# A fused attention and FFN kernel: opening reordered, masks in fp16, warm-up matmuls, values fixed up one chunk earlier

## The chip, the core and the metric

The kernel runs on one core of one Trainium2 chip. The metric is the device time in microseconds (us) of one execution. The kernel was timed several times on each chip, and medians are quoted. All runs named here are fast: none is more than 1.5% above the fastest run of its kernel.

The times of the kernel before fall into two groups, about 264.9 to 265.7 us and about 266.8 to 268.2 us, so its median moves between 265.4 and 267.5 us with the share of each group. The profiled run of it took 267.2 us, so its trace is of the slower group. What sets the groups apart was not found. Experiments are therefore compared in microseconds with the median of the changed kernel (240.16 us, and 240.05 us when it was run again in another call), and not by their ratios to the kernel before.

## The reference, cut to what matters

```python
# q, k, v: (4 batches, 8 heads, 768 positions, 64) fp32;  w_in (512, 2048), w_out (2048, 512)
scores = q @ k.T / 8
keep   = (key < 8) | ((0 <= rel) & (rel < 96))        # 8 global keys, and a band of 96
bias   = -slope[h] * where(is_global & ~is_local, 96, abs(rel))
a      = softmax(where(keep, scores + bias, -1e9))
x      = (a @ v), heads side by side                  # 3072 tokens x 512
out    = (relu(x @ w_in) ** 2) @ w_out                # fp32, 3072 x 512
```

The kernel computes the exponential of the scores and multiplies it by a mask, `exp(-slope * distance)`, built once and zero where `keep` is false.

## The kernel before

The 3072 tokens are cut into 12 chunks of 256, three to a batch. Each chunk goes through these jobs, each a Python closure that emits instructions; in the traces each engine runs what is emitted for it in that order (TensorE's weight loads may go ahead): before, the first copy of q waited on VectorE until 7.38 us, behind the masks, though its transposes started at 5.64 us. The jobs are:

- `load`: q, k, v from HBM, issued by GpSimd (names of tiles: `sq`, `sk`, `sv`);
- `turn_q`, `turn_k`: TensorE transposes (`trq`, `trk`), ScalarE or VectorE copies to `qx`, `kx`, VectorE copies beside them (`kb` for chunks that are not the first of a batch);
- `fix_v`: VectorE copies the values into `vodd`, and, for the eight chunks that are not the first of a batch ("shifted" below), also into `veven`, with rows of the chunk before and the global keys:

```python
        nc.vector.tensor_copy(out=odd[:, hh, :, 0:D], in_=cut(ck.sv, slice(0, P)))       # L244
        if ck.u != 0:
            nc.vector.tensor_copy(out=odd[0:GP, ...], in_=glob)                          # L248
            nc.vector.tensor_copy(out=even[0:HP, ...], in_=cut(ck.sv, slice(0, HP)))     # L249
            nc.vector.tensor_copy(out=even[HP:P, ...], in_=cut(pre.sv, slice(HP, P)))    # L250
            nc.vector.tensor_copy(out=even[HP:HP + GP, ...], in_=glob)                   # L251
```

- `att[c][0..7]`: two batches of scores (`sp` on TensorE, `ex` on ScalarE, `phat = ex * mask` on VectorE); four attends (`av` on TensorE, then `rec` and `tm`, the normalisation, on VectorE); two `to_x` (`trx` on TensorE, `xt` on ScalarE);
- `f1(c)`: first FFN matmul (`hps`), relu (`hr`, ScalarE), square (`h`, VectorE); `f2(c)`: second FFN matmul (`yps`), copy, store.

FFN jobs and attention jobs of a later chunk are interleaved by `place(main, side, slots)`, which puts each side job ahead of the main job of that number. The opening and the first phase read:

```python
        fill_ident(); load(0, q); fill_index(); load(0, k); load(0, v)     # fill_index: 8 index fills on GpSimd
        load_w_in(0, 512); load(1); ...                                    # cut: the other loads
        fill_masks(); fill_dist(0, 2, 0)              # VectorE, fp32
        fill_decay(0, 2, 0, 4)                        # ScalarE: mask of heads 0 to 3
        run([turn_q(0) and turn_k(0) in halves, att[0][0],
             fill_decay(0, 2, 4, 8), fix_v(0), att[0][2], att[0][1],       # heads 4 to 7
             fill_even(), att[0][3], att[0][6], turn_q(1), att[0][4],      # even masks, VectorE
             turn_k(1), att[0][5], att[0][7], fill_decay(2, 3, 0, 8)])
        run(place(f1(0), [fix_v(1)] + [att[1][i] for i in ORDER] + prep(2),
                  [1, 0, 2, 3, 4, 5, 6, 6, 7, 6, 7]))
        ...                                           # cut: f1(1) with chunk 2, f2(0) with chunk 3
        for c in range(1, NC):                        # steady stages: f2(c) and f1(c+1) in turn
            side = [fix_v(c + 3)] + [att[c + 3][i] for i in ORDER];  slots = [2, 0, 4, 5, 7, 8, 11, 12, 15]
```

The softmax here doesn't subtract the row's maximum and nothing guards it: scores larger than these inputs give would overflow.

## Time and profile before

| | before |
|---|---|
| median | 265.4 us (265.04 to 267.4, 4 runs) |
| profiled span | 265.4 us |
| TensorE busy | 224.8 us |
| TensorE idle | 40.6 us, of it about 13.7 before the first `hps`, 3.7 after the last matmul |

From the page of the kernel before: the busy line of TensorE, and its busy share and granted clock in 40 equal slices of the span (one digit a slice, in tenths).

```profile
...
PE 224.8 (85%) x2208; PEld 155.6 (59%) x2208; DVE 156.4 (59%) x410; ACT 143.8 (54%) x255; POOL 39.7 (15%) x57
...
PE   1335579498878998999998989999989979999994
...
PEclk9999759979999999999999999999999999999999
...
```

The row "PE" shows that the second half is full and that the first quarter is not. The row "PEclk" shows a lowered clock in several slices there.

The stretches view of the kernel before gives, for each stretch, its length, the busy time and the number of instructions of TensorE, its weight loads, VectorE, ScalarE and GpSimd, then the granted clock, the DMA share and GB/s.

```profile
...
30.00:40.00 10.00, 5.61 (x50) 3.91 (x48) 6.09 (x17) 3.75 (x8) 3.40 (x4) 0.67 1.30 203
50.00:60.00 10.00, 7.02 (x74) 5.32 (x72) 6.41 (x19) 4.77 (x10) 0.00 (x0) 0.83 0.39 39
80.00:100.00 20.00, 18.85 (x194) 13.27 (x193) 14.04 (x36) 12.26 (x23) 2.63 (x3) 1.00 0.74 101
160.00:180.00 20.00, 20.00 (x212) 14.03 (x212) 12.21 (x32) 11.97 (x21) 0.00 (x0) 1.00 0.08 28
...
```

TensorE is busy 18.85 of 20 us at 80 us, but all 20 at 160 us. Between 30 and 40 us it is busy 5.61 us of 10, at a mean clock of 0.67.

The waits view of TensorE for the kernel before lists who waited for what: total us, times, longest.

```profile
...
PE av L291 <- DVE veven L251: 8.2, 8, 1.2
...
PE av L291 <- DVE vodd L248: 6.1, 6, 3.1
...
PE av L291 <- DVE vodd L244: 4.2, 2, 3.0
...
```

Here `av` waits for `fix_v`, 18.5 us behind the three copies L251, L248 and L244; 3.0 us of the last line lie in the opening. VectorE is only 59% busy in the whole, but its queue is in order: the copies for a chunk are emitted just ahead of the attend that needs them.

The chain of work that ended last shows the clock's effect (start, us, what):

```profile
...
35.34 1.71 PE hps L335 x8
37.48 1.72 PE hps L335 x8
...
86.11 0.87 PE hps L335 x8
...
```

Eight `hps` matmuls take 1.71 us near 36 us and 0.87 later. The opening, from the timeline of the kernel before (start, us, engine, line, operation, tiles, count; in brackets idle time ahead and what ended it):

```profile
...
3.79 0.90 POOL L184 DMA_DIRECT2D sk<-in_k_dram  x1
...
6.48 0.98 DVE L147 TENSOR_SCALAR dist<-dist,fill 128x512 f32<-128x512 f32 x1
...
7.38 0.40 DVE L198 COPY qx<-trq 128x512 f16<-128x512 f16 x1
7.54 1.28 ACT L151 ACT_TABLE_LOAD   x1 [7.54 <-DVE dist L147]
...
12.92 2.21 ACT L151 ACTIVATE mask<-dist 128x512 f16<-128x512 f32 x4
...
18.29 0.35 DVE L135 TENSOR_SCALAR dist<-dist_94,shift 128x256 f32<-128x256 f32 x1
...
20.46 0.42 DVE L298 TENSOR_TENSOR tm<-av,rec 128x256 f16<-128x256 f32 x1
...
26.87 3.35 PE L335 MATMUL hps<-xt,w_in_sb 128*128 128x256 f16 x16
...
```

The masks hold VectorE until 7.4 us, and only then can it copy the transposed q. The exponentials of heads 4 to 7 (12.92), the even masks (from 18.29) and then the normalisation (20.46) come before the first `hps` at 26.87 us.

### The profile page before, as it was taken

To read this page: it belongs to the slowest core of one execution; us is meant where nothing else is said; L and a number is where in the kernel's file an instruction comes from. 1 tells how busy PE (TensorE), PEld (TensorE's weight loads), DVE (VectorE), ACT (ScalarE), POOL (GpSimd) and SP (SyncE) were. 2 spreads that over 40 slices of the span, in tenths; PEclk is the share of its full clock that TensorE was granted. 3 is DMA by queue.
4 is the path that set the end of the run, shared out by engine and by line. 5 is a ranking of instruction groups with operands and counts; after the bars stand their busy time and mean duration, and the time that the engine had idled before them with its cause. 6 is when DMAs were issued, how large, how long until landed. Compare 5 with 4: busy or idle time off the path is not lost.

```text
span 265.4 us, 5380 instructions
## 1 busy us (share of the span) xinstructions
PE 224.8 (85%) x2208; PEld 155.6 (59%) x2208; DVE 156.4 (59%) x410; ACT 143.8 (54%) x255; POOL 39.7 (15%) x57
## 2 busy tenths in 40 slices
PE   1335579498878998999998989999989979999994
PEld 1224357376445765777765757777657656766651
DVE  6765357656668659547667677476486565333331
ACT  0854819549455754765674575567637635333310
POOL 8843322103031201201210200000000000000000
PEclk9999759979999999999999999999999999999999
DMA  5999999904849194284724811011101101111112
GB/s 51 175 190 198 199 202 181 154 3 45 110 52 154 41 118 42 51 111 42 103 61 77 81 40 42 0 42 41 42 0 42 40 2 41 42 40 40 42 40 79
DMA packets 45144, 20.26 MB, mean 76 GB/s; under 512 B 37952, under 2 KB 42048, under 8 KB 45120
## 3 DMA queue, kind: packets, MB, share of 16 engines
q0 software_dynamic: 41664, 13.63, 46.3%
q1 hardware_dynamic: 3456, 6.29, 6.2%
q8 instruction: 17, 0.28, 0.4%
q14 instruction: 7, 0.06, 0.1%
HBM read 27.26 MB, written 6.29 MB: 126 GB/s over the span
## 4 chain that ended last, share of the span: by engine, by line
PE 62%; DVE 17%; ACT 16%; issue 3%; POOL 1%; POOLq 0%; ACTq 0%
PE yps L347 26%; PE hps L335 25%; ACT ex L274 9%; PE av L291 5%; DVE phat L277 3%; PE sp L267 3%; ACT hr L338 2%; PE trx L310 2%; DVE vodd L244 2%; ACT mask L151 2%; DVE veven L251 1%; DVE veven L250 1%; DVE vodd L248 1%; PE trk L211 1%; ACT kx L213 1%
## 5 line engine op out<-in xcount | busy, mean ns | idle before, releaser
L335 PE MATMUL hps<-xt,w_in_sb 128*128 128x256 f16 x768 | 103.8, 281 | 0.0
L338 ACT ACTIVATE hr<-hps 128x512 f16<-128x512 f32 x96 | 58.6, 614 | 80.2 <-PE hps L335 80.0
L335 PEld LDWEIGHTS <-w_in_sb 128*128 128x128 f16 x768 | 73.8, 100 | 19.4 <-issue 0.3
L274 ACT ACTIVATE ex<-sp 128x512 f16<-128x512 f32 x96 | 49.5, 605 | 11.7 <-PE sp L267 11.7
L277 DVE TENSOR_TENSOR phat<-ex,mask 128x1024 f16<-128x1024 f16 x48 | 33.2, 692 | 28.6 <-ACT ex L274 28.6
L291 PEld LDWEIGHTS <-phat 128*128 128x128 f16 x384 | 19.0, 102 | 28.0 <-issue 9.1
L291 PE MATMUL av<-vodd,phat 128*128 128x65 f16 x256 | 19.9, 203 | 10.8 <-DVE vodd L248 6.1
L298 DVE TENSOR_TENSOR tm<-av,rec 128x256 f16<-128x256 f32 x48 | 20.4, 424 | 1.7
L312 ACT CAST xt<-trx 128x512 f16<-128x512 f32 x24 | 14.6, 607 | 10.0 <-PE trx L310 9.9
L184 POOL DMA_DIRECT2D sq<-in_q_dram x12 | 10.7, 896 | 60.7 <-PE trq L196 58.0
L351 DVE COPY y<-yps 128x512 f32<-128x512 f32 x24 | 16.4, 685 | 5.4 <-PE yps L347 5.4
L267 PE MATMUL sp<-qx,kx 64*128 64x128 f16 x256 | 15.6, 234 | 3.9 <-DVE kx L225 1.4
L291 PE MATMUL av<-veven,phat 128*128 128x65 f16 x128 | 11.5, 197 | 8.2 <-DVE veven L251 8.2
L267 PEld LDWEIGHTS <-kx 64*128 64x128 f16 x256 | 10.5, 102 | 11.4 <-issue 8.0
L184 POOL DMA_DIRECT2D sk<-in_k_dram x12 | 10.7, 891 | 39.8 <-PE trk L211 35.5
L310 PE MATMUL trx<-perm,tm 128*128 128x128 f16 x96 | 10.2, 223 | 6.6 <-DVE tm L298 6.6
L310 PEld LDWEIGHTS <-tm 128*128 128x128 f16 x96 | 7.1, 99 | 10.7 <-DVE tm L298 8.1
L196 PE MATMUL trq<-ident,sq 128*128 128x128 f16 x96 | 8.2, 234 | 5.6 <-DVE loc L143 5.6
L198 ACT COPY qx<-trq 128x1024 f16<-128x1024 f16 x11 | 11.4, 1038 | 1.9 <-PE trq L196 1.9
L213 ACT COPY kx<-trk 128x1024 f16<-128x1024 f16 x11 | 11.7, 1060 | 0.3 <-PE trk L211 0.3
L184 POOL DMA_DIRECT2D sv<-in_v_dram x12 | 10.7, 893 | 2.8 <-DMA w_out_sb<-in_moe_w_out_dram 1.3
L196 PEld LDWEIGHTS <-sq 128*128 128x128 f16 x96 | 6.8, 106 | 5.8 <-DMA sq<-in_q_dram 5.6
(85 smaller groups left out, 280.0 us busy)
## 6 DMA issues: line engine op xcount, KB each, us to landing
out_dram<-y SPq DMA_DIRECT2D x24, 256.0 KB, 2.0
sq<-in_q_dram POOLq DMA_DIRECT2D x12, 256.0 KB, 4.5
sk<-in_k_dram POOLq DMA_DIRECT2D x12, 256.0 KB, 5.6
sv<-in_v_dram POOLq DMA_DIRECT2D x12, 256.0 KB, 6.5
w_in_sb<-in_moe_w_in_dram POOLq DMA_DIRECT2D x4, 512.0 KB, 12.0
w_out_sb<-in_moe_w_out_dram POOLq DMA_DIRECT2D x4, 512.0 KB, 17.8
```

Of the source, the lines that this page charges most:

```text
L184: nc.gpsimd.dma_start(out=dst, in_=src[ck.b, :, ck.u * CH:(ck.u + 1) * CH, :].rearrange("h (p e) d -> p h (e d)", e=2))
L196: nc.tensor.transpose(out=trp[:, h, :], in_=ck.sq[:, h, :], identity=ident)
L267: nc.tensor.matmul(sp[ek][:, e, s, :], lhsT=ck.keys[rr][rows, h, :], rhs=ck.q[rows, 1 - ek:3 - ek, h, rr * HP:(rr + 1) * HP], start=True, ...
L274: nc.scalar.activation(out=ex[:, ek].rearrange("p e c -> p (e c)"), in_=sp[ek].rearrange("p e s c -> p (e s c)"), func=AF.Exp, scale=scale)
L277: later.append(lambda: nc.vector.tensor_tensor(out=phat, in0=ex, in1=mask[:, :, 2 * a:2 * a + 2, k0:k0 + 2, :].rearrange("p k e s c -> p k ...
L291: nc.tensor.matmul(av[:, e, rr, :], lhsT=phat[:, ek, e, s * P:(s + 1) * P], rhs=ck.vals[rr][:, 2 * a + e, ek, 0:D + 1], start=ek == 0, sto ...
L298: nc.vector.tensor_tensor(out=tm.rearrange("p r e d -> p e r d"), in0=av[:, :, :, 0:D], in1=rec[:, :, :, None].to_broadcast([P, 2, 2, D]), ...
L310: nc.tensor.matmul(trx[:, i, rr, :], lhsT=ck.tm[2 * g + i][:, rr, :, :], rhs=perm, start=True, stop=True)
L335: nc.tensor.matmul(hps[:, m2, :], lhsT=w_in_sb[:, kk, m * P:(m + 1) * P], rhs=ck.xt[:, kk, :], start=kk == 0, stop=kk == NCT - 1)
L338: nc.scalar.activation(out=hr, in_=hps, func=AF.Relu)
L347: nc.tensor.matmul(ck.yps, lhsT=ck.h2[:, m, j * P:(j + 1) * P], rhs=w_out_sb[:, m, :], start=m == 0, stop=m == NFT - 1)
L351: nc.vector.tensor_copy(out=y, in_=ck.yps)
```

## The change

The intent is to shorten the opening and to take `fix_v` off the path of TensorE. The diff, cut to its core (the stated cuts are declarations, and the new mask algebra, which builds the same masks with fewer steps, and a change to `place`, which now also takes side jobs behind the last main job):

```diff
-    BIG = 1.0e5
+    BIG = 30000.0
-    sv_p = ctx.enter_context(tc.tile_pool(name="svp", bufs=6))
+    sv_p = ctx.enter_context(tc.tile_pool(name="svp", bufs=7))
-    dist = const.tile([P, 2, 3, P], FP32, name="dist")
+    dist = const.tile([P, 2, 3, P], FP16, name="dist")
     ... (the other mask tiles likewise; even masks now in the same operations)
+        nc.scalar.activation(out=tiny, in_=tiny, func=AF.Exp)      # table load at the start
+    def warm(n):
+        wps = bank([P, 512], "warm")
+        for _ in range(n):
+            nc.tensor.matmul(wps, lhsT=zero[:, 0:P], rhs=zero, start=True, stop=True)
     ...
-        fill_ident()
-        load(0, q)
+        fill_small()
         fill_index()                                               # 3 index fills, was 9 with that of fill_ident
-        load(0, k)
-        load(0, v)
+        load(0)
         load_w_in(0, 512)
         load(1)
+        fill_dist()
     ...
-        fill_decay(0, 2, 0, 4)
+        fill_decay(0, 2, 0, 8)
-        run([lambda: turn_q(0, 0, 4, dve), ...
-             att[0][0], lambda: fill_decay(0, 2, 4, 8), lambda: fix_v(0), att[0][2], att[0][1],
-             lambda: fill_even(), att[0][3], att[0][6], lambda: turn_q(1), att[0][4],
-             lambda: turn_k(1), att[0][5], att[0][7], lambda: fill_decay(2, 3, 0, 8)])
-        run(place(f1(0), [lambda: fix_v(1)] + [att[1][i] for i in ORDER] + prep(2),
-                  [1, 0, 2, 3, 4, 5, 6, 6, 7, 6, 7]))
+        run([lambda: warm(6), lambda: turn_q(0, 0, 4, dve), ...
+             att[0][0], lambda: (fix_v(0), fill_perm()), att[0][1], att[0][2], att[0][3],
+             lambda: turn_q(1), att[0][6], lambda: turn_k(1), att[0][4], att[0][5],
+             lambda: fix_v(1), att[0][7], lambda: fill_decay(2, 3, 0, 4), att[1][0],
+             lambda: fill_decay(2, 3, 4, 8)])
+        run(place(f1(0), [att[1][i] for i in ORD1] + prep(2) + [lambda: fix_v(2)],
+                  [2, 3, 4, 5, 6, 7, 8, 6, 7, 7]))
     ... (the next two phases likewise)
-                side = [lambda c=c: fix_v(c + 3)] + [att[c + 3][i] for i in ORDER]
-                slots = [2, 0, 4, 5, 7, 8, 11, 12, 15]
+                side = [att[c + 3][i] for i in ORDER]
+                slots = [0, 4, 5, 7, 8, 11, 12, 15]
-                side += prep(c + 4)
-                slots += [2, 9]
+                side += prep(c + 4) + [lambda c=c: fix_v(c + 4)]
+                slots += [2, 9, 13]
```

More of the change, by code (lines that the diff above doesn't have):

```diff
@@ L21, in place @@
     out = []
-    for i, f in enumerate(main):
-        out += [g for g, s in zip(side, slots) if s == i]
-        out.append(f)
+    for i in range(len(main) + 1):
+        out += [g for g, s in zip(side, slots) if s == i] + main[i:i + 1]
     return out
@@ L53 @@
     slopes = [2.0 ** (-8.0 * (h + 1) / H) for h in range(H)]
-    BIG = 1.0e5
+    BIG = 30000.0
     GP = NG // 2
     assert NG % 2 == 0 and NG <= 32 and NL <= P - 32 and 2 * D == P
-    assert BIG * min(slopes) > 150.0
+    assert BIG * min(slopes) > 110.0
     const = ctx.enter_context(tc.tile_pool(name="const", bufs=1))
     stage_p = ctx.enter_context(tc.tile_pool(name="stage", bufs=3))
-    sv_p = ctx.enter_context(tc.tile_pool(name="svp", bufs=6))
+    sv_p = ctx.enter_context(tc.tile_pool(name="svp", bufs=7))
     qk_p = ctx.enter_context(tc.tile_pool(name="qkp", bufs=3))
@@ L83 @@
     mask = const.tile([P, 2, H, 3, P], FP16, name="mask")
-    dist = const.tile([P, 2, 3, P], FP32, name="dist")
-    dist0 = const.tile([P, 2, P], FP32, name="dist0")
-    loc = const.tile([P, 2, 3, P], FP32, name="loc")
-    ge0 = const.tile([P, 2, 3, P], FP32, name="ge0")
-    jmp = const.tile([P, P], FP32, name="jmp")
-    pidx = const.tile([P, 1], FP32, name="pidx")
-    upper = const.tile([P, 1], FP32, name="upper")
+    dist = const.tile([P, 2, 3, P], FP16, name="dist")
+    off = const.tile([P, 2, 3, P], FP16, name="off")
@@ L91, with fill_index @@
+    cut = const.tile([P, 2, 3, P], FP16, name="cut")
+    jmp = const.tile([P, P], FP16, name="jmp")
+    jmp2 = const.tile([P, P], FP16, name="jmp2")
     shift = const.tile([P, 1], FP32, name="shift")
     thr = const.tile([P, 1], FP32, name="thr")
-    pmod = const.tile([P, 1], FP32, name="pmod")
     fill = const.tile([P, 2], FP32, name="fill")
-    def fill_ident():
+    zero = const.tile([P, 512], FP16, name="zero")
+    tiny = const.tile([P, 1], FP32, name="tiny")
+    def fill_index():
@@ L97, in fill_ident @@
         nc.gpsimd.iota(jmp, pattern=[[1, P]], base=0, channel_multiplier=-1,
                        allow_small_or_imprecise_dtypes=True)
-        nc.vector.tensor_scalar(out=ident, in0=jmp, scalar1=0.0, scalar2=None,
-                                op0=ALU.is_equal)
-    def fill_index():
-        nc.gpsimd.iota(pidx, pattern=[[0, 1]], base=0, channel_multiplier=1,
+        nc.gpsimd.iota(dist[:, 0, 0, :].rearrange("p (e c) -> p e c", e=2),
+                       pattern=[[1, 2], [2, HP]], base=0, channel_multiplier=-2,
@@ L104, in fill_index @@
                        allow_small_or_imprecise_dtypes=True)
-        for kind, base in ((0, 0), (1, P)):
-            for ek in range(2):
-                nc.gpsimd.iota(dist[:, ek, kind, :].rearrange("p (e c) -> p e c", e=2),
-                               pattern=[[1, 2], [2, HP]], base=base - ek,
-                               channel_multiplier=-2, allow_small_or_imprecise_dtypes=True)
-        for ek in range(2):
-            nc.gpsimd.iota(dist0[:, ek, :].rearrange("p (e c) -> p e c", e=2),
-                           pattern=[[1, 2], [2, HP]], base=-ek, channel_multiplier=-2,
-                           allow_small_or_imprecise_dtypes=True)
@@ L114, in fill_index, with fill_small @@
-        nc.gpsimd.iota(jmp, pattern=[[1, P]], base=0, channel_multiplier=-2,
+        nc.gpsimd.iota(jmp2, pattern=[[1, P]], base=0, channel_multiplier=-2,
                        allow_small_or_imprecise_dtypes=True)
-    def fill_masks():
+    def fill_small():
         V = nc.vector
-        V.tensor_scalar(out=upper, in0=pidx, scalar1=float(HP), scalar2=None, op0=ALU.is_ge)
-        V.tensor_scalar(out=shift, in0=upper, scalar1=float(CH), scalar2=None, op0=ALU.mult)
-        V.tensor_scalar(out=thr, in0=upper, scalar1=-float(P - 1), scalar2=None, op0=ALU.mult)
-        V.scalar_tensor_tensor(out=pmod, in0=upper, scalar=-float(HP), in1=pidx,
-                               op0=ALU.mult, op1=ALU.add)
-        V.tensor_scalar(out=fill[:, 0:1], in0=pidx, scalar1=float(GP), scalar2=BIG - NL,
-                        op0=ALU.is_ge, op1=ALU.mult)
-        V.tensor_scalar(out=fill[:, 1:2], in0=pmod, scalar1=float(GP), scalar2=None,
-                        op0=ALU.is_lt)
-        V.tensor_tensor(out=fill[:, 1:2], in0=fill[:, 1:2], in1=upper, op=ALU.mult)
-        V.tensor_scalar(out=fill[:, 1:2], in0=fill[:, 1:2], scalar1=-(BIG - NL),
-                        scalar2=BIG - NL, op0=ALU.mult, op1=ALU.add)
-        V.tensor_scalar(out=fill, in0=fill, scalar1=float(NL), scalar2=None, op0=ALU.add)
-        V.tensor_scalar(out=perm, in0=jmp, scalar1=thr, scalar2=None, op0=ALU.is_equal)
@@ L134, in fill_even @@
-    def fill_even():
-        nc.vector.tensor_scalar(out=dist[:, :, 2, :], in0=dist0, scalar1=shift,
-                                scalar2=None, op0=ALU.add)
-        fill_dist(2, 3, 1)
-    def fill_dist(k0, k1, f):
-        V = nc.vector
-        d, l, g = dist[:, :, k0:k1, :], loc[:, :, k0:k1, :], ge0[:, :, k0:k1, :]
-        V.tensor_scalar(out=g, in0=d, scalar1=0.0, scalar2=None, op0=ALU.is_ge)
-        V.scalar_tensor_tensor(out=l, in0=d, scalar=float(NL), in1=g,
-                               op0=ALU.is_lt, op1=ALU.mult)
-        V.scalar_tensor_tensor(out=d, in0=d, scalar=fill[:, f:f + 1], in1=l,
-                               op0=ALU.subtract, op1=ALU.mult)
-        V.tensor_scalar(out=d, in0=d, scalar1=fill[:, f:f + 1], scalar2=None, op0=ALU.add)
+        V.memset(tiny, 0.0)
@@ new lines, in fill_small, with fill_dist @@
+        nc.scalar.activation(out=tiny, in_=tiny, func=AF.Exp)
+        V.memset(zero, 0.0)
+        V.memset(fill, BIG)
+        V.memset(fill[0:GP, 0:1], float(NL))
+        V.memset(fill[HP:HP + GP, 1:2], float(NL))
+        V.memset(shift[0:HP], 0.0)
+        V.memset(shift[HP:P], float(CH))
+        V.memset(thr[0:HP], 0.0)
+        V.memset(thr[HP:P], -float(P - 1))
+    def fill_dist():
+        V = nc.vector
+        V.tensor_scalar(out=ident, in0=jmp, scalar1=0.0, scalar2=None, op0=ALU.is_equal)
+        V.tensor_scalar(out=dist[:, 1, 0, :], in0=dist[:, 0, 0, :], scalar1=1.0,
+                        scalar2=None, op0=ALU.subtract)
+        V.tensor_scalar(out=dist[:, :, 1, :], in0=dist[:, :, 0, :], scalar1=float(P),
+                        scalar2=None, op0=ALU.add)
+        V.tensor_scalar(out=dist[:, :, 2, :], in0=dist[:, :, 0, :], scalar1=shift,
+                        scalar2=None, op0=ALU.add)
+        V.tensor_scalar(out=cut, in0=dist, scalar1=0.0, scalar2=float(NL - 1), op0=ALU.max,
+                        op1=ALU.min)
+        V.tensor_tensor(out=off, in0=dist, in1=cut, op=ALU.not_equal)
+        for k0, k1, f in ((0, 2, 0), (2, 3, 1)):
+            V.tensor_scalar(out=off[:, :, k0:k1, :], in0=off[:, :, k0:k1, :],
+                            scalar1=fill[:, f:f + 1], scalar2=None, op0=ALU.mult)
+        V.tensor_tensor(out=dist, in0=cut, in1=off, op=ALU.max)
@@ L152, in fill_decay, with fill_perm @@
                                  func=AF.Exp, scale=-slopes[h])
+    def fill_perm():
+        nc.vector.tensor_scalar(out=perm, in0=jmp2, scalar1=thr, scalar2=None,
+                                op0=ALU.is_equal)
+    def warm(n):
+        wps = bank([P, 512], "warm")
+        for _ in range(n):
+            nc.tensor.matmul(wps, lhsT=zero[:, 0:P], rhs=zero, start=True, stop=True)
     later = []
@@ L394 @@
         load(3)
-        fill_masks()
-        fill_dist(0, 2, 0)
-        fill_decay(0, 2, 0, 4)
+        fill_decay(0, 2, 0, 8)
         att = [attention(c) for c in range(NC)]
         dve = nc.vector.tensor_copy
-        run([lambda: turn_q(0, 0, 4, dve), lambda: turn_q(0, 4, 8, dve),
+        run([lambda: warm(6), lambda: turn_q(0, 0, 4, dve), lambda: turn_q(0, 4, 8, dve),
              lambda: turn_k(0, 0, 4, dve), lambda: turn_k(0, 4, 8, dve),
-             att[0][0], lambda: fill_decay(0, 2, 4, 8), lambda: fix_v(0), att[0][2], att[0][1],
-             lambda: fill_even(), att[0][3], att[0][6], lambda: turn_q(1), att[0][4],
-             lambda: turn_k(1), att[0][5], att[0][7], lambda: fill_decay(2, 3, 0, 8)])
-        run(place(f1(0), [lambda: fix_v(1)] + [att[1][i] for i in ORDER] + prep(2),
-                  [1, 0, 2, 3, 4, 5, 6, 6, 7, 6, 7]))
+             att[0][0], lambda: (fix_v(0), fill_perm()), att[0][1], att[0][2], att[0][3],
+             lambda: turn_q(1), att[0][6], lambda: turn_k(1), att[0][4], att[0][5],
+             lambda: fix_v(1), att[0][7], lambda: fill_decay(2, 3, 0, 4), att[1][0],
+             lambda: fill_decay(2, 3, 4, 8)])
+        ORD1 = (2, 3, 1, 6, 4, 5, 7)
+        run(place(f1(0), [att[1][i] for i in ORD1] + prep(2) + [lambda: fix_v(2)],
+                  [2, 3, 4, 5, 6, 7, 8, 6, 7, 7]))
         load(4)
-        run(place(f1(1), [lambda: fix_v(2)] + [att[2][i] for i in ORDER] + prep(3),
-                  [1, 0, 2, 3, 4, 5, 6, 6, 7, 6, 7]))
+        run(place(f1(1), [att[2][i] for i in ORDER] + prep(3) + [lambda: fix_v(3)],
+                  [0, 2, 3, 4, 5, 6, 7, 8, 6, 7, 7]))
         load(5)
-        run(place(f2(0), [lambda: fix_v(3)] + [att[3][i] for i in ORDER] + prep(4),
-                  [1, 0, 2, 3, 4, 5, 6, 6, 7, 6, 7]))
+        run(place(f2(0), [att[3][i] for i in ORDER] + prep(4) + [lambda: fix_v(4)],
+                  [0, 2, 3, 4, 5, 6, 7, 8, 6, 7, 7]))
         for c in range(1, NC):
```

## The prediction

> **What bounds the kernel now.** TensorE: 224.8 of 265.4 us busy (busy table), mean granted clock 0.974. The stretches view puts it at 94 to 95% from 80 to 200 us and at 100% from 220 us to the last matmul (about 261.7). The 40.6 us of idle time lie elsewhere: about 13.7 us before the first FFN phase (26.3 us), 3.7 us after the last matmul, about 23 us between. The waits view of TensorE names most of that middle part: fixed-up values, `veven` 8.2 us (8 waits), `vodd` L248 6.1 us (6), `vodd` L244 4.2 us (3.0 of it in the opening): about 15.5 us in the middle. The slices also show a lowered clock behind the long gaps: 0.86, 0.67 and 0.83 in 20-30, 30-40 and 50-60 us. Eight `hps` matmuls there take 1.72 us in the chain against 0.87 later; I count about 5 us lost. This agrees with the Trainium skill, "TensorE: Matmul & The Clock Gate", Part 1 (half clock after an idle window, full after a busy one).
>
> **What the change does, costed from the timeline.**
> 1. Opening. Before, `sk` is issued at 3.79 us behind six iotas and lands at 8.4; now q, k, v follow each other from about 1.6 us (0.9 us an issue), so k lands near 7.2 and the whole load stream shifts by about 1.2 us. Masks held VectorE until 7.4 us though q was transposed at 6.2; in fp16 and with fewer steps I estimate 3 us of VectorE work, done near 5. (The skill, "VectorE: DVE Perf Modes", perf-mode tier table: 16-bit single-source operations are quicker than fp32.) The table load of 1.28 us leaves the chain. First scores near 9.0 instead of 10.4.
> 2. Between scores and FFN: `mask` exponentials of heads 4 to 7 (2.2 us) no longer sit between the two batches of `ex`; the even masks (2.0 us VectorE, 18.3-20.3) no longer sit ahead of the normalisation. First FFN phase starts near 20.5-21 instead of 26.3: 5.5 us.
> 3. `fix_v` (2.2 to 2.4 us of VectorE per chunk) runs one chunk ahead: the 15.5 us of waits go, and most of the clock loss (3.5 of 5 us). Half of this lies in the first two FFN phases, about 7 us in the six later stages with a shifted chunk (1.2 us each).
> 4. Warm-up matmuls, about 2.6 us while TensorE is idle anyway: I expect under 1 us either way.
>
> Sum 5.5 + 15.5 + 3.5 = 24.5 us. Taken back: the first FFN phase becomes bound by ScalarE (my sum from the durations: about 14.8 us of exponentials, relus and copies against 11.6 of TensorE work); the last `to_x` of early stages comes one slot later, just ahead of its consumer; `fix_v` at the stage's end delays squares and y copies. About 2.5 us.
>
> **Predicted: 243.5 us, range 238 to 249** (8%). Faster by over 2%: 0.97; within 2%: 0.02; slower: 0.01.
>
> **Right if:** the first `hps` begins at 20-22 us; waits of `av` on `vodd`/`veven` fall below 2 us in total; no slice after 30 us below clock 0.95; busy TensorE falls to about 218-221 us and its idle time to about 23; stretches from 80 to 200 us are over 98% busy. The first relu of the first phase comes behind the even masks' exponentials, and that phase is paced by ScalarE.
>
> **Wrong if:** VectorE then becomes the new wait in the steady stages (squares, `tm`, y behind `fix_v`); TensorE stays at half clock through the first phase; loads of chunk 2 or 3 (near 27-30 and 41-44 us) become the wait, since they are needed some 10 us earlier than before; 16-bit mask operations are slowed by the DMA issues of GpSimd next to them (some copies in the opening took 0.6-0.8 us instead of 0.4).

## The result, and the profile after

The changed kernel takes 240.16 us (median of 4 runs, 239.92 to 241.05) against 265.4 us. The ratio of the fast runs is 0.904, with a 95% interval of 0.899 to 0.909. It is the mean time of one kernel's fast runs over that of the other's of the same rounds, so not quite the ratio of the medians. The time lies inside the stated range, 3.3 us under the predicted centre.

The page of the changed kernel, the same lines:

```profile
...
PE 221.9 (93%) x2214; PEld 155.1 (65%) x2214; DVE 152.4 (64%) x409; ACT 143.6 (60%) x256; POOL 38.6 (16%) x51
...
PE   4666988979899999999999999999999999999993
...
PEclk9999999999999999999999999999999999999998
...
```

TensorE has 17.3 us idle in a span of 239.2 us instead of 40.6 in 265.4. Part of its 221.9 us of work is new: 2.7 us are the warm-up matmuls, which the prediction's 218 to 221 us had left out (without them it is 218.4 us, third experiment). The last slice's clock of 0.8 belongs to the time after the last matmul.

The stretches view of the changed kernel:

```profile
...
30.00:40.00 10.00, 8.02 (x111) 6.84 (x109) 8.99 (x26) 8.70 (x16) 3.14 (x5) 1.00 1.38 200
50.00:60.00 10.00, 9.99 (x102) 5.53 (x100) 6.44 (x15) 6.44 (x12) 1.50 (x2) 1.00 1.01 121
80.00:100.00 20.00, 20.00 (x207) 14.17 (x205) 12.16 (x30) 13.83 (x26) 2.96 (x4) 1.00 0.52 80
160.00:180.00 20.00, 20.00 (x211) 14.30 (x209) 14.12 (x43) 13.04 (x23) 0.00 (x0) 1.00 0.07 28
...
```

In the stretches of 80 to 100 and 160 to 180 us TensorE is now busy all the time, and in none of the four stretches is the clock below 1.00. In 30 to 40 us it is busy 8.02 us, beside VectorE at 8.99 and ScalarE at 8.70: both are busier than TensorE there.

The waits view of TensorE of the changed kernel:

```profile
...
PE trx L304 <- DVE tm L292: 4.7, 7, 1.7
PE trq L190 <- DMA sq<-in_q_dram: 2.0, 1, 2.0
PE av L285 <- DVE vodd L238: 1.5, 1, 1.5
PE sp L261 <- DVE kx L207: 1.3, 1, 1.3
...
```

What is left of the waits of `av` on `fix_v` is the 1.5 us of chunk 0 in the opening. The longest item is now `trx` behind the normalisation `tm`.

The opening, from the timeline of the changed kernel:

```profile
...
5.09 0.56 DVE L132 TENSOR_TENSOR dist<-cut,off 128x768 f16<-128x768 f16 x1
5.75 4.27 ACT L136 ACTIVATE mask<-dist 128x512 f16<-128x512 f16 x8 [3.52 <-DVE dist L132]
...
6.02 1.04 PE L190 MATMUL trq<-ident,sq 128*128 128x128 f16 x8 [2.05 <-DMA sq<-in_q_dram]
...
9.31 0.76 DVE L207 COPY kx<-trk 128x512 f16<-128x512 f16 x2
...
9.79 1.56 PE L261 MATMUL sp<-qx,kx 64*128 64x128 f16 x25 [1.31 <-DVE kx L207]
...
18.66 0.29 DVE L216 COPY kb<-kx 128x512 f16<-128x512 f16 x1 [1.19 <-ACT kx L207]
...
20.21 0.42 DVE L292 TENSOR_TENSOR tm<-av,rec 128x256 f16<-128x256 f32 x1
...
21.99 3.59 PE L329 MATMUL hps<-xt,w_in_sb 128*128 128x256 f16 x16
...
```

The masks end on VectorE at 5.65 us. ScalarE computes all eight masks from 5.75 us, then goes into `ex`. The first `sp` starts at 9.79 us, only 0.6 us earlier than before (10.36 us). The first `hps` starts at 21.99 us, 4.9 us earlier. Its sixteen matmuls still take 3.59 us, about the 3.35 us of before.

To see where the time came from, one can take the start of the q transposes of a chunk as a milestone in all four traces (timeline of TensorE), the columns "opening only" and "fix-up only" being the first two experiments below:

| milestone, us | before | opening only | fix-up only | changed |
|---|---|---|---|---|
| first `hps` | 26.87 | 20.97 | 27.38 | 21.99 |
| `trq` of chunk 2 | 42.90 | 36.93 | 37.35 | 31.34 |
| `trq` of chunk 3 | 60.81 | 52.46 | 51.73 | 44.47 |
| `trq` of chunk 5 | 80.91 | 72.97 | 70.50 | 63.66 |
| `trq` of chunk 11 | 192.01 | 184.05 | 175.79 | 168.96 |
| span | 265.4 | 257.4 | 246.1 | 239.2 |

From before to changed, 4.9 us are gained by the first `hps`, 12.4 more by chunk 5, and 9.0 in the steady stages after it. In these, a stage used to take 17.56 us when the chunk in it was the first of a batch and 18.85 to 19.06 us when it was shifted. In the changed kernel every one of them takes 17.54 to 17.56 us. In the second trace of the changed kernel every milestone comes 1.2 to 1.4 us earlier than in the last column, so differences of a microsecond between single traces say little here; the stages from chunk 5 on take the same time in both.

### The profile page after: what moved, and what is told of

It is laid out like the page before. It is cut to its first block, busy times and chain, and to the rows that moved or that the text cites. A ratio compares the mean times of both kernels' runs of the same rounds, so it can differ in the third digit from the quotient of the medians.

```text
span 239.2 us, 5383 instructions
## 1 busy us (share of the span) xinstructions
PE 221.9 (93%) x2214; PEld 155.1 (65%) x2214; DVE 152.4 (64%) x409; ACT 143.6 (60%) x256; POOL 38.6 (16%) x51
## 4 chain that ended last, share of the span: by engine, by line
PE 82%; ACT 8%; DVE 6%; DMA 2%; issue 1%; POOL 0%; POOLq 0%
PE yps L341 34%; PE hps L329 33%; PE sp L261 5%; PE av L285 4%; ACT ex L268 4%; PE trx L304 2%; DMA sq<-in_q_dram 2%; PE trq L190 2%; PE trk L205 2%; ACT hr L332 2%; DVE tm L292 1%; ACT kx L207 1%; ACT qx L192 1%; DVE qx L195 1%; DVE qx L196 1%
## 5 line engine op out<-in xcount | busy, mean ns | idle before, releaser
L329 PE MATMUL hps<-xt,w_in_sb 128*128 128x256 f16 x768 | 101.1, 276 | 0.0
L341 PE MATMUL yps<-w_out_sb,h 128*128 128x512 f16 x384 | 97.3, 379 | 0.0
L329 PEld LDWEIGHTS <-w_in_sb 128*128 128x128 f16 x768 | 72.7, 99 | 18.5 <-issue 0.2
L333 DVE TENSOR_TENSOR h<-hr 128x512 f16<-128x512 f16 x96 | 40.5, 422 | 43.9 <-ACT hr L332 43.4
L341 PEld LDWEIGHTS <-h 128*128 128x128 f16 x384 | 34.8, 98 | 26.6
L285 PE MATMUL av<-vodd,phat 128*128 128x65 f16 x256 | 18.5, 201 | 2.5 <-DVE vodd L238 1.5
L261 PE MATMUL sp<-qx,kx 64*128 64x128 f16 x256 | 15.5, 232 | 2.9 <-DVE kx L207 1.3
```

The costliest lines, as they stand in the source:

```text
L261: nc.tensor.matmul(sp[ek][:, e, s, :], lhsT=ck.keys[rr][rows, h, :], rhs=ck.q[rows, 1 - ek:3 - ek, h, rr * HP:(rr + 1) * HP], start=True, ...
L285: nc.tensor.matmul(av[:, e, rr, :], lhsT=phat[:, ek, e, s * P:(s + 1) * P], rhs=ck.vals[rr][:, 2 * a + e, ek, 0:D + 1], start=ek == 0, sto ...
L329: nc.tensor.matmul(hps[:, m2, :], lhsT=w_in_sb[:, kk, m * P:(m + 1) * P], rhs=ck.xt[:, kk, :], start=kk == 0, stop=kk == NCT - 1)
L333: later.append(lambda: nc.vector.tensor_tensor(out=ck.h2[:, 2 * i:2 * i + 2, :], in0=hr, in1=hr, op=ALU.mult))
L341: nc.tensor.matmul(ck.yps, lhsT=ck.h2[:, m, j * P:(j + 1) * P], rhs=w_out_sb[:, m, :], start=m == 0, stop=m == NFT - 1)
```

## The experiments

Twelve runs were made, the last of them of the changed kernel itself. All are correct: they give the reference's output.

### 1. The opening alone

Edit: the changed kernel with `fix_v` back in the slots of before.

```diff
-             lambda: fix_v(1), att[0][7], ...
+             att[0][7], ...
-        run(place(f1(0), [att[1][i] for i in ORD1] + prep(2) + [lambda: fix_v(2)], [2, ..., 8, 6, 7, 7]))
+        run(place(f1(0), [lambda: fix_v(1)] + [att[1][i] for i in ORD1] + prep(2), [1, 2, ..., 8, 6, 7]))
     ... (likewise in the other phases; steady stages: fix_v(c + 3) at slot 2 again)
```

> The changed kernel with the values fixed up as late as before (same slots as before), the new opening kept. Theory (three nearly additive parts: opening about 5 us, waits on the fixed-up values about 15 us, clock about 4 us): 255 to 259 us, waits of av on vodd and veven back to 12-16 us in total, clock dips behind the gaps back. Rival (the earlier start of the FFN carries the gain and the waits would mostly have been absorbed, or just move to another engine): 243 to 249 us.

Measured: 259.87 us (4 runs, 259.17 to 259.97; before 265.7). By medians that is 5.8 us for the whole new opening; against the two groups of before (medians 265.0 and 267.6) it is 5.2 or 7.8 us. It is 19.7 us of loss against the changed kernel, just over the expected range of 255 to 259 us. The waits of TensorE:

```profile
...
PE av L285 <- DVE veven L245: 8.2, 8, 1.3
PE av L285 <- DVE vodd L242: 6.4, 6, 3.5
...
```

The longest `vodd` wait is even longer than before (3.5 us against 3.1); that the FFN gets there sooner and meets the same late copies is the likely reason. The rival, that the early start carries the gain, falls.

### 2. The earlier fix-up alone

Edit: the kernel before with `svp` at 7 buffers and `fix_v` one chunk further ahead; old masks, loads and order, no warm-up.

```diff
-             lambda: turn_k(1), att[0][5], att[0][7], ...
+             lambda: turn_k(1), att[0][5], lambda: fix_v(1), att[0][7], ...
     ... (fix_v(2), fix_v(3), fix_v(4) at slot 7 of the three phases, fix_v(c + 4) at slot 13 of a steady stage)
```

> The kernel before with only the values fixed up one chunk further ahead; old masks, old load order, no warm-up. Theory: 265.4 less 15 us of waits less 3 to 4 us of clock = 246 to 249 us, stretches 80-200 us over 98% busy on TensorE. Rival (opening carries the gain): 258 to 262 us.

Measured: 247.67 us (4 runs, 247.24 to 247.91), 18.0 us less than the median of before (17.4 or 20.0 us against its two groups). The stretches view of this run:

```profile
...
80.00:200.00 120.00, 120.00 (x1261) 85.07 (x1260) 82.45 (x223) 76.34 (x136) 8.96 (x11) 1.00 0.33 54
...
```

TensorE is busy for all 120 us. So the steady stages owe their gain to this part alone. The two parts, 5.8 and 18.0 us, add up to 23.8, while both together give 25.2 (265.4 to 240.16). The rest of 1.4 us is smaller than the distance of the two groups of the kernel before, and nothing is read from it. A comparison without the kernel before is steadier: from this run to the changed kernel (247.67 to 240.16) the new opening is worth 7.5 us on top of the earlier fix-up. Not every wait behind `fix_v` is gone here: two waits of `sp`, 2.8 us together, are put down to `veven`.

### 3. No warm-up matmuls

```diff
-        run([lambda: warm(6), lambda: turn_q(0, 0, 4, dve), ...
+        run([lambda: turn_q(0, 0, 4, dve), ...
```

> The changed kernel without the six warm-up matmuls. Theory (they run in idle time and end 2 us before the first load lands; the transposes behind them still take the time of the slow clock): within 0.5 us of 240.2. Rival (they bring the full clock earlier): 1 to 2 us slower than 240.2.

Measured: 240.35 us (6 runs, 239.81 to 241.2), the same as the changed kernel. In this trace and in the first of the changed kernel the eight q transposes take 1.04 us, without and with the six dummies (in the second trace of the changed kernel, 0.62 us). In the time of the kernel the six contribute nothing that shows.

### 4. The clock loss of before, without the waits

Edit: the kernel before with dummy matmuls ahead of the attends that wait.

```diff
-        run(place(f1(0), [lambda: fix_v(1)] + [att[1][i] for i in ORDER] + prep(2), [1, 0, 2, ...
+        run(place(f1(0), [lambda: fix_v(1), lambda: warm(13)] + [att[1][i] for i in ORDER] + prep(2), [1, 2, 0, 2, ...
     ... (warm(8) at the same place of f1(1); a zeroed tile for them)
```

> The kernel before with dummy matmuls (13 and 8 of 512 columns) in the two long gaps of the first two FFN phases, ahead of the attend that waits; the waits themselves stay. Splits the lost clock from the waits. Theory (about 4 us of the time in these phases is matmuls at half clock): 261 to 263 us, slices of 30-60 us at full clock, hps groups of 8 at 0.87 us in the chain. Rival (lowered clock costs nothing of its own, since TensorE waits there anyway): 264.5 to 267 us.

Measured: 263.49 us (4 runs, 263.22 to 263.85), 2.2 us less than the median of before (265.7). The profiled runs differ by 3.7 us (span 261.7 against 265.4), because that of before is of its slower group. The stretches view of this run:

```profile
...
30.00:40.00 10.00, 8.35 (x89) 5.65 (x87) 7.36 (x19) 6.00 (x13) 3.62 (x4) 1.00 1.30 203
50.00:60.00 10.00, 8.29 (x115) 6.80 (x116) 7.42 (x20) 6.65 (x13) 0.88 (x1) 1.00 0.44 45
...
```

The clock stays at 1.00 where it was 0.67 and 0.83, and the waits of `av` on `veven` remain (7.9 us in 8 waits). So a lowered clock did cost time of its own: 2.2 us by medians (ratio 0.983 to 0.996), 1.5 or 4.1 us against the two groups of before, and not 5. It is also the smaller part: the 18 us of the second experiment are mostly waits.

### 5. The loads of chunk 0 apart again

```diff
-        load(0)
+        load(0, q)
+        for i in range(7):
+            nc.gpsimd.iota(spare[:, i, :], pattern=[[1, P]], base=0, channel_multiplier=-1, ...)
+        load(0, k)
+        load(0, v)
```

> The changed kernel with seven spare index fills put on GpSimd between the load of q and that of k of chunk 0, as much as stood there before (about 1.4 us). Theory (k is the last thing that the first scores wait for, through its copy on VectorE): k lands about 1.2 us later, the first scores at about 10.6 instead of 9.8, and 0.5 to 1.2 us of it arrive at the end: 240.7 to 241.4 us. Rival (VectorE, busy with the q copies until 9.3, hides the later k): within 0.3 us of 240.2.

Measured: 240.22 us (5 runs, 239.69 to 241.26), the same as the changed kernel. The timeline of TensorE in this run:

```profile
...
8.46 1.03 PE L206 MATMUL trk<-ident,sk 128*128 128x128 f16 x8 [1.54 <-DMA sk<-in_k_dram]
9.86 1.57 PE L262 MATMUL sp<-qx,kx 64*128 64x128 f16 x25 [0.36 <-DVE kx L208]
...
```

The k transposes come 1.0 us later (8.46 instead of 7.44), but the first `sp` only 0.07 us later (9.86 instead of 9.79). VectorE is busy with the copies of q until 9.3 us anyway. The rival holds: issuing the loads in a row gains nothing here.

### 6. Masks in fp32

Edit: `dist`, `off`, `cut`, `jmp` and `jmp2` declared FP32 instead of FP16; same operations.

> The changed kernel with the four mask and index tiles in fp32, same operations, same order. Theory (VectorE ends the masks about 1.5 us later, near 7, so the q copies and the mask exponentials start later): first scores at 10.3 to 11, the end 0.5 to 1.5 us later: 240.7 to 241.7 us. Rival (16 bits are what saves most of the mask time): mask work on VectorE over 6 us instead of 3.7, end 2 to 4 us later.

Measured: 240.97 us (6 runs, 240.41 to 242.39), 0.8 to 0.9 us more, though the ranges of the two kernels overlap. The last mask operation ends on VectorE near 7.2 us instead of 5.65; the operations over 768 elements take 0.56 instead of 0.36 us (`cut`) and 0.96 instead of 0.56 us (`off`, two inputs). The first `hps` starts at 22.53 us.

### 7. Masks late again

Edit: the changed kernel with the exponentials of heads 4 to 7 between the two score batches, and the even part of `fill_dist` ahead of the second normalisation.

```diff
-        fill_decay(0, 2, 0, 8)
+        fill_decay(0, 2, 0, 4)
-             att[0][0], lambda: (fix_v(0), fill_perm()), att[0][1], att[0][2], att[0][3],
+             att[0][0], lambda: fill_decay(0, 2, 4, 8), lambda: (fix_v(0), fill_perm()), att[0][1],
+             att[0][2], lambda: fill_dist(2, 3, 1), att[0][3],
```

> The changed kernel with only the place of the masks put back: exponentials of heads 4 to 7 between the two batches of scores of chunk 0, the even masks on VectorE ahead of the second normalisation. Still fp16, still the new loads. Theory (these stood on the chain; 2.2 us of ScalarE and about 1.3 us of VectorE): first hps 2 to 3.5 us later than 22.0, end 2 to 3.5 us later: 242 to 243.7 us. Rival (the chain of chunk 0 was bound by the load stream or by k of chunk 1): first hps within 0.7 us, end within 0.7 us.

Measured: 243.33 us (6 runs, 243.12 to 244.96), 3.2 us more than the changed kernel. The first `hps`, from the timeline of TensorE:

```profile
...
25.05 3.08 PE L329 MATMUL hps<-xt,w_in_sb 128*128 128x256 f16 x16
...
```

It starts 3.1 us later than in the first trace of the changed kernel (21.99; 4.2 later than in the second), and 3.2 us arrive at the end by medians, with ranges that lie apart. Of the parts of the opening that were tested, the place of the masks is the largest.

### 8. More dummy matmuls

```diff
-        run([lambda: warm(6), ...
+        run([lambda: warm(11), ...
     ... (warm(3) ahead of att[0][0], warm(4) behind att[0][1], warm(5) behind att[0][5])
```

> The changed kernel with more dummy matmuls: 11 ahead of the first load, and 3, 4 and 5 in the later gaps of the opening, so that TensorE is nearly always busy from 1.2 us. Theory (the six of the change are too few to raise the clock, more of them do, but only a little of the opening's chain is TensorE time): transposes of eight at 0.6 instead of 1.04 us, first sixteen hps at 1.9 instead of 3.6 us, end 0.5 to 1.5 us earlier: 238.7 to 239.7 us. Rival (no effect, since ScalarE paces the first phase): within 0.3 us of 240.2.

Measured: 239.1 us (5 runs, 238.77 to 239.94), about 1 us less; ten runs of the changed kernel took 239.5 to 241.1. The timeline of TensorE:

```profile
...
1.23 4.87 PE L146 MATMUL warm<-zero 128*128 128x512 f16 x11 [1.23 <-DVE fill L108]
6.12 0.62 PE L190 MATMUL trq<-ident,sq 128*128 128x128 f16 x8
...
20.98 1.92 PE L329 MATMUL hps<-xt,w_in_sb 128*128 128x256 f16 x16
24.10 0.24 PE L285 MATMUL av<-vodd,phat 128*128 128x65 f16 x2 [1.20 <-DVE phat L271]
...
```

Here the eight q transposes take 0.62 us behind eleven dummies, and the first sixteen `hps` 1.92 us; in the first trace of the changed kernel these were 1.04 and 3.59 us. But the number of dummies ahead does not settle it. Each run left one trace: without dummies ahead, the q transposes took 1.03 to 1.04 us in all four (before, second, third and fourth run); with six, 1.03 to 1.04 us in five and 0.62 in two (first and twelfth run); with eleven, 0.62 us in two and 1.03 in one (ninth run). What decides it was not found. So that a raised clock gives the 1 us is argued and not shown. A larger gain meets a limit: `av` then waits 1.20 us for `phat`, so the next stop of the chain is not on TensorE.

### 9. A rebuilt opening

Edit, in its core:

```diff
+        fill_dist(0, 2, 0); fill_dist(2, 3, 1)        # even masks behind the others
-        load(0); load_w_in(0, 512); load(1)
+        load(0); load(1); load_w_in(0, 512)
     ... (q of chunk 2 ahead of the last part of w_in, chunk 3 ahead of w_out)
+        opening: q of heads 0 to 3, then k of heads 0 to 3, through VectorE; then heads 4 to 7; fix_v(0)
+        run([lambda: warm(11), opening, att[0][0], lambda: warm(4), att[0][1],
+             turn_1,                                  # transposes of chunk 1; VectorE's part held back
+             att[0][2], att[0][3], att[0][4], att[0][5], lambda: [f() for f in held],
+             lambda: warm(5), att[0][6], lambda: fill_decay(2, 3, 0, 2), att[0][7],
+             lambda: fill_decay(2, 3, 2, 8), lambda: fix_v(1)])
     ... (scores of chunk 1 behind the first hps; the dummies write banks that f2 uses later)
```

> An attempt at a better version from what the runs showed: even masks after the others on VectorE; q, k of the first four heads through VectorE ahead of the other four, so that the first scores start near 8.6 instead of 9.8; q and k of chunk 1 loaded ahead of the first FFN weights and turned before the first attend; the copies beside chunk 1's q and k behind the normalisations of chunk 0; the scores of chunk 1 behind the first hps; q of chunk 2 ahead of the last part of w_in, chunk 3 ahead of w_out; the dummy matmuls of the eighth run. Theory (the opening is one chain through VectorE and ScalarE and the first two phases are paced by ScalarE, whose idle time in the opening this fills): first hps at 17 to 19 instead of 22, end 2 to 4 us earlier than 240.2: 236 to 238 us. Rival (the load stream is already the bound of the first phases): first hps earlier, but waits on the loads of chunk 2 or 3 take it back, 239 to 240.5 us.

Measured: 237.0 us (6 runs, 236.64 to 238.08), 3.1 us less than the changed kernel. The first `hps` starts at 16.43 us instead of 21.99, so 2.5 us of the 5.6 us won there were given back later (1.3 of 4.4 us against the second trace of the changed kernel). It is a start with a stop: two matmuls, and the other six of this group only from 17.52 us. The waits of `av` on `phat` are 3.8 us in total, the longest 1.8 us.

### 10. The rebuilt opening, and chunk 3 turned earlier

```diff
-        run(place(f1(1), ..., [0, 2, 3, 4, 5, 6, 7, 8, 6, 7, 7]))
+        run(place(f1(1), ..., [0, 3, 4, 4, 5, 6, 7, 8, 3, 5, 7]))
```

> The ninth run, and in the second FFN phase q and k of chunk 3 turned at slots 3 and 5 instead of 6 and 7, first attends one slot later, so that the copies for chunk 3 do not stand ahead of the last normalisation on VectorE (1.5 us of wait of trx on tm near 48 us in the changed kernel). Theory: 0.7 to 1.5 us less than the ninth run. Rival (ScalarE paces the phase whatever the order): within 0.3 us of it.

Measured: 236.38 us (6 runs, 235.96 to 237.94), 0.6 us less than the ninth run, a little less than expected, and the two runs' ranges overlap. It is 3.8 us less than the changed kernel. TensorE's waits in this run:

```profile
...
PE trk L205 <- DMA sk<-in_k_dram: 1.6, 2, 0.8
...
PE trq L190 <- DMA sq<-in_q_dram: 1.4, 2, 0.8
...
```

Transposes wait for loads of two chunks now (3.0 us in all), where the changed kernel had 2.4 us of such waits, all for chunk 0. The load stream may become a bound of the opening; no run tested that.

### 11. The table load back at the first mask

Edit: the exponential of one element in `fill_small` removed.

> The changed kernel without the one-element exponential that loads ScalarE's table at the start, so that the load (1.28 us) comes at the first mask exponential. Theory (ScalarE goes without a break from the masks, 5.75 us, into the ex of chunk 0, so the table load would stand on the chain): masks end near 11.3 instead of 10.0, first hps 0.9 to 1.3 us later, end 0.8 to 1.4 us later: 241.0 to 241.6 us. Rival (the load is issued while ScalarE waits for the masks anyway, as the table does not depend on data): within 0.3 us of 240.2.

Measured: 240.47 us (6 runs, 240.32 to 241.32), 0.3 to 0.4 us more than the changed kernel, between theory and rival, and less than the spread of the changed kernel's own runs (239.5 to 241.1 us). ScalarE's timeline in this run:

```profile
...
5.74 1.28 ACT L135 ACT_TABLE_LOAD   x1 [5.74 <-DVE dist L131]
7.03 4.26 ACT L135 ACTIVATE mask<-dist 128x512 f16<-128x512 f16 x8
11.20 3.98 ACT L267 ACTIVATE ex<-sp 128x512 f16<-128x512 f32 x8
```

The table load stands at 5.74 us for 1.28 us, and `ex` starts 0.77 us later (11.20 instead of 10.43), since a pause of 0.41 us ahead of `ex` takes up a part. The first `hps` starts 0.61 us later (22.60) than in the first trace of the changed kernel, which is less than the 1.17 us between that kernel's two traces.

### 12. The changed kernel again

> The changed kernel itself, unaltered, five rounds: it was timed four times only, in another call than the experiments that differ from it by less than 1 us. Theory (what differs between calls is small): median 239.9 to 240.5 us, so that the third, fifth and eleventh run are the same within noise and the eighth is about 1 us faster. Rival: the median lies over 0.5 us away from 240.16, and the small differences must be read anew.

Measured: 240.05 us (6 runs, 239.47 to 240.98). Differences of 0.8 us and more can stand, within a few tenths of a microsecond; the 0.2 to 0.4 us of the third and eleventh runs cannot be told from noise. Its trace, of a run of 239.72 us (timeline of TensorE):

```profile
...
5.91 0.62 PE L190 MATMUL trq<-ident,sq 128*128 128x128 f16 x8 [1.95 <-DMA sq<-in_q_dram]
...
20.82 3.21 PE L329 MATMUL hps<-xt,w_in_sb 128*128 128x256 f16 x16
...
```

The kernel is the same, yet the first transposes take 0.62 us and not 1.04, the first `sp` starts at 9.37 us (9.79 in the first trace), the first `hps` at 20.82 us (21.99), and the span is 237.9 us (239.2). In this opening a difference of a microsecond between single traces therefore shows nothing by itself; the medians decide.

## Why the prediction was right or wrong

The time was right, and so was the order of the parts. The gain of 25.2 us (21.9 predicted) came out larger mainly because the steady stages gave more and less was taken back. That the sum came so close is partly luck, since the clock's term was too large and the others too small. Point by point:

- **Waits on the fixed-up values (predicted: 15.5 us of waits and 3.5 us of clock go, 2.5 us are taken back).** The second experiment shows 18.0 us for this part alone, the first a loss of 19.7 us when it is undone (both with the clock's part in them). The mechanism is shown: no wait of `av` on `vodd` or `veven` is left after chunk 0. Two terms were mis-sized. The six late stages with a shifted chunk gave 9.0 us and not 7: each waited 1.2 us by the waits view, but its stage was 1.3 to 1.5 us longer than the others. And little was taken back, by the balance of the sum: VectorE did not become a new limit of the steady stages, for TensorE was busy for 100% of the time from 80 to 200 us, where over 98% was predicted.
- **Clock (predicted: about 5 us lost, 3.5 us regained).** Too large by medians: the fourth experiment keeps the waits and fills them, for 2.2 us. The count came from a trace of the slower group (267.2 us), against which the same run gives 4.1 us, so how much too large stays open. Its statement that no slice after 30 us falls below 0.95 held but for the last slice, after the last matmul. The Trainium skill ("TensorE: Matmul & The Clock Gate", Part 1) says that the clock is halved after an idle window and full after a busy one; the traces agree, with eight `hps` at 1.71 us behind a gap and 0.87 elsewhere.
- **Opening (predicted: 5.5 us).** The first experiment shows 5.8 us by medians, the second 7.5 us for the opening on top of the earlier fix-up, and the first `hps` came at 21.99 us (20.82 in the second trace), within 20 to 22. But its reasons were only partly right, so that the sum fits is in part luck. Masks late: 3.2 us, as argued. 16 bits: 0.8 us, in the direction that the skill gives ("VectorE: DVE Perf Modes", perf-mode tier table), 0.36 against 0.56 us for one operation. Loads in a row: nothing (fifth run; eight index fills stood between the loads of q and k, not the six of the prediction), because VectorE's copies of q and not the landing of k release the first scores. The predicted first scores "near 9.0" came at 9.79 us (9.37 in the second trace), behind the same copies. Table load: "leaves the chain" was true, but the effect measured, 0.3 to 0.4 us, is within noise, and far below the 1.28 us that the load lasts; the skill ("ScalarE: Activation LUTs", What ACT_TABLE_LOAD costs) has 1283 ns for the load. These parts, each undone in the changed kernel, add up to about 4.4 us, and the opening there is worth 7.5; the remaining 3 us were not taken apart. The smaller number of mask operations and the new order of jobs, with scores of chunk 1 ahead of the first FFN, are untested rivals for them.
- **Warm-up (predicted: under 1 us).** Right: 0.2 to 0.3 us, within noise. Whether they raise the clock differed between two traces of the same kernel.
- **First phase paced by ScalarE.** The first relu came at 25.97 us, right behind the last even masks, as predicted. ScalarE was busy 8.35 us of the 10 from 20 us on and 8.70 of the next 10, and VectorE 8.99 of 10 us from 30 us on. The eighth run supports that TensorE is not the pace there: its first sixteen `hps` ended at 22.90 us and those of the twelfth run's trace at 24.03 us, yet its span (238.2 us) was no shorter than that one's (237.9). That ScalarE alone is the pace was not shown.
- **Idle time of TensorE (predicted about 23 us).** 17.3 us. Of the difference, about 2.5 us are the time by which the profiled run (241.05 us) beat the centre, and 2.7 us are the warm-up matmuls, which fill idle time without use.

## What to carry to other kernels

An engine that is 59% busy can still hold up the busiest one: in an in-order queue, work that depends only on early data should be emitted a stage ahead of its consumer, at a place where nobody waits for what stands behind it. In an opening, find the last thing that each first step waits for, before moving anything: here a whole microsecond on a load was worth nothing and three microseconds of masks were worth three. Dummy matmuls pay only as far as the matmuls behind them are the chain, and whether they raised the clock differed here between traces of one and the same kernel: take a second trace before reading a microsecond out of one.

## What the Trainium skill lacked or had wrong

- "TensorE: Matmul & The Clock Gate", Part 1: it gives about 3.4 us of busy time to full clock. These runs neither confirm nor refute the figure: behind six dummies of 2.74 us the eight transposes took 1.04 us in one trace of the changed kernel and 0.62 us in the other, behind eleven of 4.87 us they took 0.62 us in the eighth run and 1.03 us in the ninth. What it lacks: the recorded clock of the changed kernel reads 1.00 from 0 to 20 us in the first trace, while its matmuls there take the times of the slow clock (transposes at 1.04 us); in the second trace it reads 0.50 from 8 to 16 us, with the same 1.04 us. The page does warn that clock events can be unreliable; at the start of a trace, read the durations.
- "ScalarE: Activation LUTs", What ACT_TABLE_LOAD costs: it adds a drain of about 1380 ns to the 1283 ns of the load. In the eleventh run the first mask exponential starts at 7.03 us, 0.01 us after the end of the load (5.74 and 1.28 us); no such drain stands there. The page states the drain for a switch to a different set; whether the first load of an execution, with ScalarE idle ahead of it, counts as one was not tested.
